# A recurrence with two gated feed-forward layers: TensorE's order in the first three chunks written as a timetable

## The chip, the core and the metric

The kernel runs on one core of a Trainium2 chip. TensorE (PE) multiplies matrices, PEld loads its weights, VectorE (DVE), ScalarE (ACT) and GpSimd (POOL) do the elementwise work, and SyncE (SP) issues the DMAs. Each engine works through its own instructions in a fixed order, which is set when the kernel is built. The metric is the time of one execution in microseconds (us).

## What is computed

The attention part is a recurrence over 768 steps for each of 4 batches x 8 heads, with a 40 x 40 state. It is followed by two gated layers over 3072 tokens (320 to 1536 to 320), all in fp32:

```python
for t in range(S):
    y[:, :, t] = np.einsum('bhd,bhde->bhe', rt, state)
    Sa = np.einsum('bhde,bhe->bhd', state, at)
    state_decay = state * wt[:, :, None, :] - np.einsum('bhd,bhe->bhde', Sa, bt)
    state = state_decay + np.einsum('bhd,bhe->bhde', vt, kt)
...
g = x @ w_gate; val = x @ w_val
x = (g * sigmoid(g)) * val @ w_out          # first layer
x = sigmoid(x @ w_gate) * (x @ w_val) @ w_out   # second layer, its own weights
```

## The kernel before

The recurrence is cut into 12 chunks of 64 steps, and all 32 heads of a chunk are worked on together. A chunk m goes through these stages, each a Python generator whose `yield`s mark its steps:

- `prep_a(m)`: the decay products of the chunk's steps. For chunks 0 to 3 they are scans on DVE, transposed on PE (`dtp`, L153) and copied out (`pn`, L404); for chunk 0 this is in `first()`. Later chunks read them from DRAM, where `powers` has put them. Then the scaled a is transposed (`tp` L356, copied to `lq` at L456), and four **key groups** follow: transposition `tp` L356, ACT's copy `kbt` L467, the key products `kps` L471, ACT's copies into `bn` L480 and L481, DVE's masked copy into `lq` L483.
- `prep_b(m)`: the inverse of a unit triangular matrix from `bn`. For chunks 0 to 2 it is `halves`: DVE solves 16-row blocks (L539 to L564) and PE joins them (`hps` L573, L586); for later chunks it is `whole`: DVE solves 32-row blocks (L497 to L521), and the result X goes through DRAM (`xd`, written at L524, read back at L526). In both PE joins the blocks of 32 by `zps` L626 and `xps` L642.
- `chain(m)`: the serial part, state to state: `qps` L677 (behind it POOL clears `lq` again, L687), `ups` L695, `sps` L706 and DVE's update of the state `sT`. It needs the inverse of chunk m and the state of chunk m - 1.
- `post(m)`: the chunk's output: `aps` L749, the mask `am` L757, `yps` L775, `ysb` L785. `cp(m)` is `chain(m)` and then `post(m)`.
- `extra(m, ys)`: the first feed-forward layer (FFN) on the finished block m: the input x (`xtp` L930), `gv` L984, activation `g` on ACT (L988), `hh` on ACT (L992), `hl` on POOL (L993), `po` L1002. Block 0 uses three of the weight tiles ("w tile 0" to "w tile 2"), later blocks five; the rest of the first layer and all of the second follow behind the recurrence. `extra(-2)` prepares w tiles 0 to 2, `extra(0)` also tiles 3 and 4 (`load_w`: DMA, ACT L882, POOL, DVE, and the ACT conversion L902).
- `powers(n)`: decay products for chunks 4 to 7 and 8 to 11. DVE clamps (L231), POOL multiplies (L228: two tiles `wp` and `wq`), and DMAs write both to DRAM (`pd`, `rd`). These two tiles lie in the same buffers as w tiles 3 and 4.

`fill()` zeroes static buffers on ACT; `marks` and `behind` put one instruction behind another of the same engine; `ends_scan` gives the chunk's total decay (`pend`). What sets the order before: `merge` draws steps from the generators by rates and offsets (QA, QB, NA, NB and so on), which gives the program's order, and the Tile scheduler then orders each engine's instructions from that order and its own estimates of when operands are ready.

## Time and profile before

| | |
|---|---|
| time, median of 3 runs | 1327.23 us (1326.39 to 1330.4) |
| the profiled execution | 1332.88 us, span 1331.2 us |
| PE busy | 1243.8 us, 93% of the span |
| DVE, ACT, POOL busy | 763.1, 598.3, 558.5 us |
| PE's mean granted clock | 0.938 |

The profile's page gives sums over the span and the span in 40 slices of 33.3 us. The views of the trace give groups of instructions, waits and timelines. L153 is line 153 of the kernel before; times are us from the start of the span. In a timeline a row is a run of equal instructions: start, length, engine, line, operation, out <- in, shape, count, and in brackets how long the engine had stood idle ahead of it and what released it. In the trace a matrix product in fp32 appears as two instructions.

### The profile page before, as it was taken

The page shows a single profiled execution, that of the slowest core. Times are in us where ns is not written, and L with a number is a line of the kernel's source. Part 1 is how long each engine was busy: PE and PEld are TensorE (multiplying, and loading weights), DVE is VectorE, ACT ScalarE, POOL GpSimd, SP SyncE. Part 2 cuts the span into 40 slices and gives each one's busy share as a digit, 9 for nine tenths or more (in the row PEclk, how much of TensorE's full clock was granted, in tenths as well). Part 3 has the DMA queues.
Part 4 walks back from the last instruction along what each step waited for, and adds up shares of the span by engine and source line. Part 5 has one row for each costly group of instructions (what it writes and reads, how often), then busy time and mean ns, then how long its engine had stood idle before and what let it go on. Part 6 is the DMA issues. An engine that isn't in the chain of part 4 may idle for free.

```text
span 1331.2 us, 34568 instructions
## 1 busy us (share of the span) xinstructions
PE 1243.8 (93%) x14209; PEld 1182.1 (89%) x14209; DVE 763.1 (57%) x1578; ACT 598.3 (45%) x1446; POOL 558.5 (42%) x767
## 2 busy tenths in 40 slices
PE   5577799999999999999899999999999999999996
PEld 4476688888888888988899999999999999999996
DVE  6768567776786678877889888733122122212221
ACT  8453464456555655655434444423333333333331
POOL 5657341222322223447777888723222222222221
PEclk7666687899999999999899999999999999999998
DMA  6644923335424533344355544221000000000000
GB/s 211 125 124 127 214 84 99 88 105 154 121 80 110 154 109 82 103 129 124 111 188 185 181 155 161 89 85 51 23 23 23 23 23 23 23 23 23 11 11 14
DMA packets 153065, 126.15 MB, mean 95 GB/s; under 512 B 100929, under 2 KB 131137, under 8 KB 152641
## 3 DMA queue, kind: packets, MB, share of 16 engines
q1 hardware_dynamic: 152896, 123.84, 32.9%
q8 instruction: 114, 1.87, 0.6%
q14 instruction: 55, 0.44, 0.1%
HBM read 92.05 MB, written 31.76 MB: 93 GB/s over the span
## 4 chain that ended last, share of the span: by engine, by line
PE 69%; DVE 14%; DMA 5%; ACT 4%; issue 3%; POOL 2%; SPq 1%; DVEq 0%; ACTq 0%; POOLq 0%
PE g L984 26%; PE po L1002 16%; PE gv L984 8%; PE tp L356 3%; PE aps L749 3%; PE kps L471 3%; PE yps L775 2%; DVE dt L887 2%; DVE ds L892 1%; DMA wt<-in_a_w_dram 1%; PE qps L677 1%; PE ups L695 1%; PE xps L642 1%; PE sps L706 1%; DVE part L517 1%
## 5 line engine op out<-in xcount | busy, mean ns | idle before, releaser
L984 PE MATMUL g<-x,w 128*128 128x256 f32 x3520 | 489.7, 282 | 2.1 <-DVE g L990 1.3
L984 PEld LDWEIGHTS g<-x,w 128*128 128x128 f32 x3520 | 458.9, 190 | 4.2 <-DVE g L990 2.1
L993 POOL TENSOR_TENSOR hl<-g,hh 128x256 fp32r<-128x256 f32 x288 | 218.9, 760 | 474.3 <-ACT hh L992 430.9
L991 DVE TENSOR_TENSOR g<-g,g 128x256 f32<-128x256 f32 x220 | 93.0, 423 | 308.2 <-PE g L984 298.6
L992 ACT CAST hh<-g 128x256 fp32r<-128x256 f32 x288 | 117.0, 406 | 268.3 <-DVE g L991 246.9
L1002 PE MATMUL po<-w,hh 128*128 128x320 f32 x1152 | 225.8, 312 | 3.6 <-ACT hh L992 3.5
L1002 PEld LDWEIGHTS po<-w,hh 128*128 128x128 f32 x1152 | 175.3, 189 | 5.3 <-ACT hh L992 4.6
L984 PE MATMUL gv<-x,w 128*128 128x256 f32 x1088 | 161.0, 298 | 3.2 <-ACT x L936 1.7
L984 PEld LDWEIGHTS gv<-x,w 128*128 128x128 f32 x1088 | 143.2, 199 | 7.1 <-ACT x L936 2.0
L1002 PE MATMUL po<-w,hl 128*128 128x320 f32 x576 | 142.0, 316 | 0.0
L988 ACT ACTIVATE g<-g 128x256 f32<-128x256 f32 x220 | 84.2, 383 | 128.4 <-PE g L984 117.4
L904 POOL TENSOR_TENSOR dt<-dt,w 128x384 f32<-128x384 f32 (+1 forms) x72 | 79.4, 1103 | 77.8 <-DVE ds L891 36.5
L1002 PEld LDWEIGHTS po<-w,hl 128*128 128x128 f32 x576 | 91.7, 189 | 1.4 <-POOL hl L993 0.5
L511 DVE TENSOR_TENSOR pr<-part,sn 128x4 f32<-128x4 f32 (+4 forms) x135 | 74.7, 553 | 3.0
L471 PE MATMUL kps<-lq,kbt 104*128 104x128 f32 x384 | 62.0, 312 | 8.1 <-DVE lq L483 6.9
L517 DVE TENSOR_REDUCE part<-pr 128x2 f32<-128x4 f32 (+4 forms) x135 | 66.8, 495 | 3.4
L483 DVE TENSOR_TENSOR lq<-kps,part 64x256 f32<-64x256 f32 x96 | 40.4, 421 | 46.2 <-ACT bn L481 43.7
L471 PEld LDWEIGHTS kps<-lq,kbt 104*128 104x128 f32 x384 | 54.1, 217 | 10.9 <-issue 7.1
L356 PE MATMUL tp<-ident,part 128*104 128x128 f32 x288 | 50.7, 298 | 12.9 <-ACT pend L168 6.7
L749 PE MATMUL aps<-rbd,ut 104*128 104x128 f32 x384 | 57.1, 292 | 3.6 <-DVE am L757 2.0
L902 ACT CAST w<-dt 128x384 fp32r<-128x384 f32 (+1 forms) x72 | 35.6, 495 | 54.3 <-DVE dt L887 47.3
L480 ACT ACTIVATE bn<-kps 32x256 f32<-32x256 f32 x96 | 35.8, 373 | 53.6 <-PE kps L471 44.1
(171 smaller groups left out, 1788.9 us busy)
## 6 DMA issues: line engine op xcount, KB each, us to landing
raw<-in_w_dram SPq DMA_DIRECT2D x48, 384.0 KB
xd<-x SPq DMA_DIRECT2D x12, 896.0 KB
x<-xd SPq DMA_DIRECT2D x12, 896.0 KB
raw<-in_w_dram SPq DMA_DIRECT2D x24, 320.0 KB
ld<-in_a_kb_dram SPq DMA_DIRECT2D x22, 320.0 KB
ld<-rd SPq DMA_DIRECT2D x32, 160.0 KB
pn<-pd SPq DMA_DIRECT2D x32, 160.0 KB
ld<-in_a_a_dram SPq DMA_DIRECT2D x12, 320.0 KB
```

Source lines behind the costliest of these rows:

```text
L356: t = nc.tensor.transpose(ps[0 : x.shape[1], n, :], x, ident)
L471: nc.tensor.matmul(kps[:, n].rearrange("p h t -> p (h t)"), lhsT=kbt[0:PW, n, :], rhs=lq[m % 3][0:PW, 4 * g4 + n].rearrange("p h t -> p (h ...
L511: nc.vector.tensor_tensor(out=o, in0=xs[:, 0:kk, None, 0:n].to_broadcast([P, kk, 2, n]), in1=sn[:, None, n : n + 2, 0:n].to_broadcast([P, ...
L517: nc.vector.tensor_reduce(out=xs[:, 0:kk, n : n + 2], in_=o, axis=AX.X, op=ALU.add)
L749: nc.tensor.matmul(aps[:, n, h2], lhsT=ut[0:PW, x, 2 * h2 : 2 * h2 + 2].rearrange("p u s -> p (u s)"), rhs=rbd[0:PW, x, h2].rearrange("p b ...
L904: sub(out=tf, in0=tf, in1=w.bitcast(F32), op=ALU.subtract)
L984: nc.tensor.matmul(gv[n], lhsT=p, rhs=q, start=e == 0, stop=e == len(seq) - 1)
L988: nc.scalar.activation(out=g, in_=gv[0], func=AF.Sigmoid)
L991: nc.vector.tensor_tensor(out=g, in0=gv[1], in1=g, op=ALU.mult)
L992: nc.scalar.copy(out=hh, in_=g)
L993: self.heng.tensor_tensor(out=hl, in0=g, in1=hh.bitcast(F32), op=ALU.subtract)
L1002: self.nc.tensor.matmul(ops[u], lhsT=p[:, us], rhs=q, start=first and n == 0, stop=last and n == 2)
```

## The change

The first three chunks' work on PE is no longer ordered by `merge` and the scheduler, but by a script of steps (A is `prep_a`, B `prep_b`, C `cp`, W and E the two `extra`s, P the powers; "A0:3" is three steps of A0), inside which PE keeps the order of the program. From chunk 2's `cp` on the loop with its rates goes on as before. Around it:

- of the zero fills only five are made at the start (`lq0`, `qv`, `lq1`, `sT`, `x16`), the others behind chunk 0's last copy into `bn`;
- chunk 0's `pend` product moves out of `first()` into `prep_a(0)`;
- the transposition of the next key group is queued ahead of the products of this one, `kbt` takes turns with a second pair of buffers in chunks 0 and 1, and the key products take turns over several PSUM banks: four in chunk 0, three in chunk 1, two in chunk 2, one (`mm`) from chunk 3 on; `banks()` hands out the bank `pg` too;
- chunk 0 leaves out the copies and the eight transpositions of its state, which is zero;
- in `halves` two small scalings move from ACT to DVE;
- the first of the two groups of powers has its clamps behind chunk 0's block solve.

```diff
-    def fill():
-        for t in fills:
-            nc.scalar.copy(out=t, in_=zero[(slice(None),) + (None,) * (len(t.shape) - 2)].to_broadcast(t.shape))
-        fills.clear()
+    def fill(ts, mark=None):
+        for t in ts:
+            to = nc.scalar.copy(out=t, in_=zero[(slice(None),) + (None,) * (len(t.shape) - 2)].to_broadcast(t.shape))
+            if mark:
+                behind(to, mark)
...
-    def ends_scan(m, p, ps):
+    def end_rows(p):
         nc.vector.tensor_tensor(
             out=pairs(pe)[:, 0].rearrange("p h (j c) -> p h j c", c=4),
             in0=p[:, None, :, C : C + 1].to_broadcast([P, 2, 10, 4]),
             in1=cm[:, :, None, :].to_broadcast([P, 2, 10, 4]),
             op=ALU.mult,
         )
+
+    def ends_scan(m, ps):
         nc.tensor.matmul(ps[0:PW], lhsT=pe[:, 0], rhs=hot, start=True, stop=True)
...
-            ends_scan(0, p, pt)
+            end_rows(p)
...
-            behind(clamp, "keys")
+            if n == 1:
+                behind(clamp, ("solved", 0))
...
+    early = ("lq0", "qv", "lq1", "sT")
+    fill([fills[n] for n in early] + [x16])
...
+        if m == 0:
+            ends_scan(0, ptp.tile([P, 4, P], F32, tag="tp", name="pep")[:, 0, 0:NS])
         bn = wk.tile([P, NS, C], F32, tag="bn", name="bn", bufs=2)
+        keys = {0: ((pmm, "mm"), (pzy, "zy"), (po, "po1"), (pqu, "qu")), 1: ((pmm, "mm"), (po, "po1"), (pg, "gv")), 2: ((pmm, "mm"), (pg, "gv"))}
+        keys = keys.get(m, ((pmm, "mm"),))
+        turned = tr4(lambda n: tk[:, n])
         for g4 in range(4):
             q = slice(4 * g4, 4 * g4 + 4)
-            ps = tr4(lambda n: tk[:, 4 * g4 + n], ("joined", None, "merged", None)[g4] if m == 1 else None)
-            kbt = wk.tile([P, 4, P], F32, tag="kbt", name="kbt", bufs=1)
-            nc.scalar.copy(out=kbt[0:PW], in_=ps[0:PW])
-            pool, tag = ((pmm, "mm"), (pzy, "zy"), (pqu, "qu"), (po, "po1"))[g4 if m == 0 else 0]
+            tag = "am" if m < 2 and g4 % 2 else "kbt"
+            kbt = wk.tile([P, 4, P], F32, tag=tag, name="kbt", bufs=2 if tag == "am" else 1)
+            nc.scalar.copy(out=kbt[0:PW], in_=turned[0:PW])
+            if g4 < 3:
+                turned = tr4(lambda n: tk[:, 4 * g4 + 4 + n])
+            pool, tag = keys[g4 % len(keys)]
...
-                nc.scalar.mul(out=bn[hi, q, 0:32], in_=kps[hi, :, h2, 32:64], mul=-1.0)
+                marks["keys"] = nc.scalar.mul(out=bn[hi, q, 0:32], in_=kps[hi, :, h2, 32:64], mul=-1.0)
...
-        nc.scalar.mul(out=sn, in_=full[:, :, 0:16], mul=par[:, 0:1])
+        nc.vector.tensor_scalar(out=sn, in0=full[:, :, 0:16], scalar1=par[:, 0:1], scalar2=None, op0=ALU.mult)
...
-        nc.scalar.mul(out=x16.rearrange("p r t -> p (r t)")[:, 1:256:34], in_=nk, mul=-1.0)
+        nc.vector.tensor_scalar(
+            out=x16.rearrange("p r t -> p (r t)")[:, 1:256:34], in0=nk, scalar1=-1.0, scalar2=None, op0=ALU.mult
+        )
...
-            nc.vector.tensor_scalar(out=to(0), in0=src, scalar1=sel[:, z : z + 1], scalar2=None, op0=ALU.mult)
+            marks[("solved", m)] = nc.vector.tensor_scalar(out=to(0), in0=src, scalar1=sel[:, z : z + 1], scalar2=None, op0=ALU.mult)
...
+            if m:
+                for h2 in range(2):
+                    nc.scalar.copy(out=two(Q[E40[h2], h2, sg]), in_=pairs(sT, s4)[E40[h2]])
+
+                ps = tr4(lambda n: sT[:, 4 * hb + n])
+                nc.scalar.copy(
+                    out=sd[0:PW, s4], in_=ps[0:PW].rearrange("p n (h e) -> p n h e", h=2)[..., 0:D]
+                )
...
-    merge([(prep_a(0), 1, 0)])
-    fill()
-    for t, step in ((x16, 17), (xs, 34)):
-        t = t.rearrange("p r t -> p (r t)")[:, ::step]
-        nc.gpsimd.tensor_copy(out=t, in_=odd[:, 0:1].to_broadcast([P, 16]) if step == 34 else less.to_broadcast([P, 16]))
-    nc.gpsimd.memset(tkb[2][..., D:64], 0.0)
-    start = [(prep_b(0), *QB)]
-    if NCH > 1:
-        start.append((prep_a(1), *QA))
-    merge(start)
-    for m in range(NCH + 1):
+    tokens = {
+        **{f"A{m}": prep_a(m) for m in range(4)},
+        **{f"B{m}": prep_b(m) for m in range(3)},
+        **{f"C{m}": cp(m) for m in range(2)},
+        "W": extra(-2, out),
+        "E": extra(0, out),
+        "P": all_powers(),
+    }
+
+    def run(script):
+        for x in script.split():
+            name, _, n = x.partition(":")
+            for _ in range(int(n or 1)):
+                next(tokens[name], None)
+
+    with tc.manual_schedule(engines={mybir.EngineType.PE}):
+        run("A1 A0:3 A1 A0 A1 A0 A1 A0:2 A1")
+        fill([t for n, t in fills.items() if n not in early], "keys")
+        for t, step in ((x16, 17), (xs, 34)):
+            t = t.rearrange("p r t -> p (r t)")[:, ::step]
+            nc.gpsimd.tensor_copy(
+                out=t, in_=odd[:, 0:1].to_broadcast([P, 16]) if step == 34 else less.to_broadcast([P, 16])
+            )
+        nc.gpsimd.memset(tkb[2][..., D:64], 0.0)
+        run("C0:3 A2 A1:2 B0:3 A1:5 B0 A2 B0 A2 B0 A2 B0:2 A2 C0:4")
+        run("A2 C0 A2 C0 A2 C0 A2 C0 A2 C0 A2:2 C0:3 A3 B1:3 C1:3 B1:2 W:10 P:99 B1:3 E C1:4 B2:3")
+        run("E C1 E C1 E C1 E C1:4 A3:4 B2:5 A3:9 E:19")
+    for m in range(2, NCH + 1):
         todo = []
-        if m == 0:
-            todo.append((extra(-2, out), *QW))
-            if len(groups) > 1:
-                todo.append((all_powers(), *QP))
-        if 0 <= m < NCH:
-            todo.append((cp(m), *(NP if m else QN)))
-        if 0 <= m < NCH - 1:
-            todo.append((prep_b(m + 1), *(NB if m else QC)))
-        if 2 <= m + 2 < NCH:
-            todo.append((prep_a(m + 2), *(NA if m else QD)))
-        todo.append((ahead(m), *(NX if m > 0 else QX)))
+        if m < NCH:
+            todo.append((cp(m), *NP))
+        if m < NCH - 1:
+            todo.append((prep_b(m + 1), *NB))
+        if m + 2 < NCH:
+            todo.append((prep_a(m + 2), *NA))
+        todo.append((ahead(m), *NX))
```

What stands in PE's queue around chunk 0's join (hps; in both kernels lq0 and bn of this place are chunk 0's, tkb1 and lq1 chunk 1's). Before:

```order
L356 MATMUL tp_628<-ident_58,part0_88 104x128 x4
L356 MATMUL tp_635<-ident_58,part0_88 104x128 x4
L573 MATMUL hps_325<-x1t_373,bn_227 32x16 x64
L586 MATMUL hps_325<-part1_212,pr_327 16x16 x64
L356 MATMUL tp_643<-ident_58,tkb1_90 104x128 x4
L356 MATMUL tp_661<-ident_58,tkb1_90 104x128 x4
L626 MATMUL zps_539<-x1t_536,bn_227 32x32 x32
L471 MATMUL kps_650<-lq1_210,kbt_648 128x128 x4
```

The same place now:

```order
L358 MATMUL tp_456<-ident_58,part0_88 104x128 x4
L358 MATMUL tp_494<-ident_58,tkb1_90 104x128 x4
L358 MATMUL tp_501<-ident_58,tkb1_90 104x128 x4
L479 MATMUL kps_506<-lq1_190,kbt_499 128x128 x4
L358 MATMUL tp_519<-ident_58,tkb1_90 104x128 x4
L479 MATMUL kps_524<-lq1_190,kbt_517 128x128 x4
L358 MATMUL tp_537<-ident_58,tkb1_90 104x128 x4
L479 MATMUL kps_542<-lq1_190,kbt_535 128x128 x4
L479 MATMUL kps_555<-lq1_190,kbt_553 128x128 x4
L583 MATMUL hps_463<-x1t_486,bn_244 32x16 x64
```

All four key groups of chunk 1 have moved ahead of chunk 0's hps.

The key groups of chunk 3 (lq0 and tkb0 again) in PE's queue, and chunk 2's inverse (hps_1739 before). Before, the last of the four groups:

```order
L749 MATMUL aps_2074<-rbd_199,ut_198 128x128 x4
L356 MATMUL tp_2494<-ident_58,part0_88 104x128 x4
L471 MATMUL kps_1957<-lq0_192,kbt_1955 128x128 x4
L365 MATMUL pep_2501<-ident_58,part2_86 104x16
L775 MATMUL yps_2146<-part3_197,rbd_199 64x40 x16
L775 MATMUL yps_2146<-tkb1_90,am_2063 64x40 x8
L775 MATMUL yps_2146<-tkb1_90,am_2079 64x40 x8
L573 MATMUL hps_1739<-x1t_2043,bn_1064 32x16 x64
```

Now, the end of chunk 2's inverse and the first group:

```order
L634 MATMUL zps_2209<-x1t_2206,bn_959 32x32 x32
L650 MATMUL xps_2244<-part1_208,zt_2208 32x32 x32
L358 MATMUL tp_2279<-ident_58,part0_88 104x128 x4
L358 MATMUL tp_2286<-ident_58,part0_88 104x128 x4
L702 MATMUL ups_2686<-qs_2684,part1_208 64x40
L702 MATMUL ups_2745<-qs_2743,part1_208 64x40
L702 MATMUL ups_2686<-qs_2684,part1_208 64x40 x15
L358 MATMUL tp_2294<-ident_58,tkb0_89 104x128 x4
L702 MATMUL ups_2745<-qs_2743,part1_208 64x40 x4
L358 MATMUL tp_2301<-ident_58,tkb0_89 104x128 x4
L702 MATMUL ups_2745<-qs_2743,part1_208 64x40 x11
L713 MATMUL sps_2765<-part3_195,tkb2_91 40x40
```

Chunk 3's groups stood ahead of chunk 2's hps and now begin behind chunk 2's xps; the products of the first follow directly on the last row.

ACT's queue around the first conversion of w tile 3 (w8_2311 before, w8_2369 now). Before:

```order
L480 ACTIVATE bn_1064<-kps_1126 32x256
L481 ACTIVATE bn_1064<-kps_1126 32x4x32
L902 CAST w8_2311<-dt_2314 128x384
L540 ACTIVATE sn_1740<-sn_1740,part2_86 128x256
L600 ACTIVATE part1_212<-hps_1140 16x16x16 x2
L404 COPY pn_1615<-dtp_1621 128x16x32
```

Now:

```order
L1008 ACTIVATE g_1813<-gv_1796 128x256
L747 COPY ut_196<-tp_1823 104x4x2x64
L1012 CAST hh_1814<-g_1813 128x256
L1008 ACTIVATE g_1853<-gv_1836 128x256
L922 CAST w8_2369<-dt_2372 128x384
L1012 CAST hh_1854<-g_1853 128x256
L1008 ACTIVATE g_1891<-gv_1874 128x256
```

The conversion has moved from between the solves of chunks 1 and 2 to between two steps of block 0's FFN.

## Rows read from the trace of the kernel before

**Rows 1.** The page: busy tenths and granted clock of PE in 40 slices.

```profile
PE   5577799999999999999899999999999999999996
...
PEclk7666687899999999999899999999999999999998
```

**Rows 2.** Windows: length, busy time (instructions) of the engines, PE's clock, DMA share, GB/s.

```profile
core 0: us, PE busy (x) PEld busy (x) DVE busy (x) ACT busy (x) POOL busy (x), PEclk, DMA share, GB/s
...
40.00:90.00 50.00, 31.76 (x637) 27.74 (x638) 32.45 (x66) 24.82 (x56) 28.26 (x38) 0.59 0.70 158
90.00:170.00 80.00, 58.87 (x960) 52.13 (x957) 57.36 (x116) 36.48 (x83) 46.46 (x57) 0.66 0.61 150
170.00:212.00 42.00, 38.52 (x728) 35.97 (x727) 30.42 (x69) 22.39 (x54) 16.98 (x24) 0.75 0.37 105
...
264.00:316.00 52.00, 50.05 (x763) 44.97 (x763) 39.30 (x79) 30.51 (x75) 14.81 (x20) 1.00 0.47 129
```

**Rows 3.** Waits of PE from 0 to 212: total us, times, longest.

```profile
PE dtp L153 <- ACT pn L404: 8.0, 2, 5.7
...
PE tp L356 <- ACT pend L168: 6.7, 1, 6.7
```

**Rows 4.** Timeline of PE in chunk 0 and chunk 1's keys.

```profile
23.31 1.92 PE L471 MATMUL kps<-lq,kbt 104*128 104x128 f32 x8
...
33.87 1.16 PE L471 MATMUL kps<-lq,kbt 104*128 104x128 f32 x8
...
54.11 1.90 PE L573 MATMUL hps<-x1t,bn 16*32 16x16 f32 x128 [9.19 <-DVE x1t L563]
...
73.03 2.05 PE L471 MATMUL kps<-lq,kbt 104*128 104x128 f32 x8 [2.85 <-DVE lq L483]
...
83.63 1.67 PE L706 MATMUL sps<-part,tkb 128*40 128x40 f32 x46
...
85.93 1.06 PE L471 MATMUL kps<-lq,kbt 104*128 104x128 f32 x8
```

**Rows 5.** Timeline of PE from chunk 1's inverse to chunk 3's.

```profile
121.28 0.75 PE L573 MATMUL hps<-x1t,bn 16*32 16x16 f32 x66
124.83 2.05 PE L471 MATMUL kps<-lq,kbt 104*128 104x128 f32 x8 [2.79 <-DVE lq L483]
...
142.13 1.12 PE L153 MATMUL dtp<-ident,s 128*64 128x128 f32 x8 [5.70 <-ACT pn L404]
...
168.56 0.81 PE L706 MATMUL sps<-part,tkb 128*40 128x40 f32 x32
...
184.99 1.06 PE L471 MATMUL kps<-lq,kbt 104*128 104x128 f32 x8
...
190.98 1.91 PE L573 MATMUL hps<-x1t,bn 16*32 16x16 f32 x128 [2.79 <-DVE lq L483]
...
209.04 1.92 PE L642 MATMUL xps<-part,zt 32*32 32x32 f32 x64
...
249.99 0.69 PE L642 MATMUL xps<-part,zt 32*32 32x32 f32 x32
```

**Rows 6.** Timeline of DVE: a powers' reciprocal, and chunk 3's whole solve.

```profile
127.44 0.40 DVE L246 RECIPROCAL part<-wp 128x40 f32<-128x40 f32 x1 [2.76 <-POOL wp L228]
...
190.76 1.23 DVE L497 STREAM_TRANSPOSE sn<-bn 128x1024 f32<-128x1024 f32 x1
...
200.85 0.69 DVE L505 TENSOR_TENSOR nt<-sn 128x512 f32<-128x512 f32 x1
...
221.58 0.71 DVE L521 STREAM_TRANSPOSE x1t<-part 128x512 f32<-128x512 f32 x1
```

**Rows 7.** Timeline of ACT: the first conversion of w tile 3.

```profile
139.76 0.51 ACT L902 CAST w<-dt 128x384 fp32r<-128x384 f32 x1 [5.06 <-issue]
```

**Rows 8.** Groups of POOL, 17 to 170: busy us, mean ns of one.

```profile
L228 POOL TENSOR_TENSOR wp<-wp 128x320 f32<-128x320 f32 x28 | 27.9, 997 | 2.1 <-DVE wp L231 1.4
```

**Rows 9.** Timeline of SP's queue: issue times of chunk 3's round trip.

```profile
227.30 1.31 SPq L524 DMA_DIRECT2D xd<-part  x2
232.21 2.01 SPq L526 DMA_DIRECT2D part<-xd  x4
```

More of the change, by code (lines that the diff above doesn't have):

```diff
@@ L53, in attention @@
     dr = ctx.enter_context(tc.tile_pool(name="at_dram", bufs=2, space=DRAM))
-    room, fills = {}, []
+    room, fills = {}, {}
     def static(shape, name, val=None, part=None):
@@ L74, in static @@
         if val == 0.0:
-            fills.append(t)
+            fills[name] = t
         elif val is not None:
@@ L263, in all_powers @@
             yield from powers(n)
-    lq = [static([P, NS, 2, C], "lq0", 0.0)]
-    fill()
+    lq = [static([P, NS, 2, C], f"lq{i}", 0.0) for i in range(3)]
     mask = static([P, C], "mask", 1.0, "part2")
@@ L355, in tr4 @@
             x = get(n)
-            t = nc.tensor.transpose(ps[0 : x.shape[1], n, :], x, ident)
-            if n == 0 and name:
-                behind(t, name)
+            nc.tensor.transpose(ps[0 : x.shape[1], n, :], x, ident)
         return ps
@@ L585, in halves @@
                 at = 32 * (j % 2) + 16
-                last = nc.tensor.matmul(
+                nc.tensor.matmul(
                     ps[32 * j : 32 * j + 16, q, 16:32],
@@ L593, in halves @@
                 )
-        if m == 0:
-            marks["joined"] = last
         for j in (0, 2, 1, 3):
@@ L641, in prep_b @@
                 lo, hi = slice(64 * h2, 64 * h2 + 32), slice(64 * h2 + 32, 64 * h2 + 64)
-                last = nc.tensor.matmul(
+                nc.tensor.matmul(
                     ps[lo, q],
@@ L649, in prep_b @@
                 )
-        if m == 0:
-            marks["merged"] = last
         for h2 in range(2):
@@ L665, in half @@
             sg, s4 = slice(8 * hb, 8 * hb + 8), slice(4 * hb, 4 * hb + 4)
-            for h2 in range(2):
-                nc.scalar.copy(out=two(Q[E40[h2], h2, sg]), in_=pairs(sT, s4)[E40[h2]])
-            ps = tr4(lambda n: sT[:, 4 * hb + n])
-            nc.scalar.copy(
-                out=sd[0:PW, s4], in_=ps[0:PW].rearrange("p n (h e) -> p n h e", h=2)[..., 0:D]
-            )
+            if m:
[5 more added lines that the diff above has]
+                )
             qps = pool.tile([P, 8, D], F32, tag=tag, name="qps")
```

20 lines of the change are left out of this document (8 added, 12 removed).

## The prediction

> **What bounds the kernel now.** I read the page's slices first: TensorE (PE) is nearly always busy and at full clock, except in the first five slices by its busy share and the first seven by its clock [rows 1]. The windows put figures to that: PE is busy for 31.8 of the 50 us from 40 to 90 at a granted clock of 0.59, for 58.9 of the 80 us from 90 to 170 at 0.66, for 38.5 of the 42 up to 212 at 0.75, and from 264 on for 50 of 52 at 1.00 [rows 2]. So the change works on the only stretch with much idle time in it, and what it brings forward by about 250 us is kept to the end, since PE has work all the time behind that. The list of waits names what PE stood for in that stretch: the decays' copy pn from ScalarE (ACT) 8.0 us, the first `tp` 6.7 [rows 3]; the longest single one is 9.19 us for the first inverse's x1t from VectorE (DVE) [rows 4]. The timelines of PE, DVE, ACT and SyncE (SP) give the milestones that I shift below. The profiled execution took 1332.88 us (span 1331.2 and 1.68 around it), 5.65 us over the median of 1327.23; I work out a shift in its time and apply it to the median.
>
> **The shift is read at one place:** chunk 3's last inverse product, xps, which PE starts at 249.99 us [rows 5]. Up to there both orders have the same chunks, key groups and feed-forward (FFN) tiles ahead of it to within about 3 us of PE work, which I count as zero and keep for the range.
>
> **1. Chunk 0.** Before, chunk 1's first transpositions are done at 54.11 − 9.19 = 44.9 and PE idles until hps starts at 54.11 [rows 4]. The timetable places chunk 1's four key groups into that hole, ahead of hps. Chunk 0's own four groups took from 23.31 to 35.03, so 11.7 us at the low clock [rows 4]; from 46 on that ends at 58 to 63, and hps starts 4 to 9 us later than before. x1t itself comes earlier, since two scalings move from ACT to DVE and the powers' clamps wait for the solve (my guess: 49 instead of 54), but this no longer decides. In return hps to the end of sps holds no key group any more. It took from 54.11 to 85.30, 31.2 us, and in it lay three key products of 2.05 us, one with a 2.85 us wait, and two dozen transpositions, about 6 us by the same half clock [rows 4]: 15 us, which leaves 16; chunk 2's decay transpositions, now inside, give 6 to 10 of it back. Chunk 0's state is then done at 80 to 89, for 85.3: nothing gained, but chunk 1's keys are complete 24 us earlier (58 to 63 for 87 [rows 4]). The other edits here (smaller fills, eight transpositions of a zero state left out) act on the 6.7 us that PE waits for the first `tp` [rows 3]; they are worth 0 to 3 us at the front, covered by the same hole, and without that cover at most these 3 us; I count nothing.
>
> **2. Chunk 2's keys, then chunk 1.** The timetable finishes chunk 2's keys right behind chunk 0's state, at about 110 (four groups of 4 to 5 us from 90 on). Before, they lay between chunk 1's products: chunk 1's hps starts at 121.28 and its sps ends at 169.37, 48.1 us [rows 5]. In this lay two of the key products (2.05 us, one with a 2.79 us wait), some 8 us of decay transpositions with their 5.70 us wait [rows 5], and some 8 us of FFN and of chunk 3's keys: 28 to 30 us, so about 19 without, of which I take 22 to 26. With hps at 115, sps ends at 137 to 141, some 30 us earlier. This is the large gain of the change.
>
> **3. FFN of block 0 and the rest of chunk 1.** These now run by themselves, and three engines' queues stand in their way. On POOL the first `hl` stands behind 27 of the 29 multiplications of the second group of powers. These can't start before chunk 1's qps, since the clearing of lq1 behind qps stands ahead of them in POOL's queue (about 116); 27 of 1.0 us [rows 8] end at 143. On ACT the conversion of w tile 3 stands between two steps of the FFN, and it waits for the DMAs that write the first powers' tile out of the same buffer. Before, it started at 139.76, 12.3 us after the reciprocal that ends this tile (127.44), with ACT idle for 5.06 us ahead of it [rows 6, 7]. That tile is now done 21 multiplications behind 116, at 137 to 145 with other work between them, and the conversion runs at 150 to 158; everything behind it on ACT (the second `hh`, chunk 1's copies) waits, and PE with it. On SP, chunk 2's load of v stands behind the same writes. From there one and a half FFN tiles, the output copies and chunk 1's second half are left, some 15 us of PE work at the low clock: 165 to 173, I take 171. Of the 30 us gained, up to half is lost here.
>
> **4. Chunk 2's inverse.** hps to xps took from 190.98 to 210.96, 20.0 us, with other products inside [rows 5]; by itself, the waits between its products now open, 12 to 16. It is done at 183 to 187: 24 to 28 us earlier than before.
>
> **5. Chunk 3's keys, the step that decides.** Before, chunk 3's four key groups lay between chunk 1's state and block 0's FFN and were done at 186.05 [rows 5]; DVE began chunk 3's whole solve at 190.76 [rows 6]. The timetable places them behind chunk 2's xps. They have one PSUM bank, so each group goes transposition, ACT copy, product, ACT and DVE copies in turn. At the pace of chunk 0 (11.7 us and the last mask) this is 14 us: the solve starts at 199 to 203, which is **8 to 12 us later** than before, although everything ahead of it is 24 to 28 us earlier. With a 2.79 us wait, as at 124.83 [rows 5], at three of the groups it would be 207 to 211.
>
> From there to X: before, L497 at 190.76, the last transposition at 221.58, the write to DRAM issued at 227.30, the reads issued until 234.22 [rows 6, 9]: 43.5 us. In this lie 8.9 us in which L505 waited (from 191.99 to 200.85 [rows 6]) and 5 in which SP's queue held the write back; both can go, neither must. So 30 to 44, and the landing; I take 40. With a start at 201, X is there at 241, and xps can run 9 us before its 249.99: **−9**.
>
> **The rivals.** *A, the forecast:* X decides, and two thirds of the lead are handed back: −4 to −20. *B, the lead goes entirely:* the solve starts at 205 to 212 and X takes 41 to 45 us: 246 to 254, within 4 us of before. For it: no step ahead of 190 speeds this solve, and one bank serves all four groups. *C, slower:* the powers, the conversion behind their DMA writes and the FFN behind the conversion slip in a row. It decides from a solve start later than 213 on (213 + 41 is 4 us behind 249.99). If lq1 is cleared at 128 instead of 116, each later step slips by 12, the solve starts at 211 to 215 and X is there 43 to 45 us later, at 254 to 260; with the mask waits of 8 us on top, at 268 at worst. I price it at **+4 to +15**. For it: ACT, POOL and SP work off their queues in order, and the trace shows this very stall (5.06 us [rows 7]). Against it: the first group of powers, 29 multiplications of 1.0 us [rows 8] behind the solve at 49 and the weights' work between them, is out of POOL's way by about 90. *D, a larger gain:* the solve's two idle spans go, X takes 31 us and isn't waited for, and PE closes up. Before, PE needed 39 us from the end of chunk 2's xps to chunk 3's xps (210.96 to 249.99 [rows 5]); with chunk 3's keys added, some 9 us, 48 from 185 on gives 233: −17, and up to −25 where the denser stretch runs at the higher clock. PE's stretches with the higher busy share show the higher clock (0.59 at 64%, 0.66 at 74%, 0.75 at 92% [rows 2]), and a key product takes 2.05 us in the one and 1.06 in the other [rows 4]. [...] *E, the order isn't what the script says:* the instruction order of the changed kernel shows the moves on PE, so it has no chance of its own.
>
> **How the numbers follow.** A 0.44, B 0.20, C 0.24, D 0.12. The median less 9 gives 1318. The range goes up to 1338 (C's +11) and down to 1302 (D's −25), which leaves a little under 0.2 outside. About 0.3% (4 us) is what a measurement of this kernel can tell from no change: faster 0.56 (A and D), same 0.20 (B), slower 0.24 (C).
>
> **What would show it.** Step 1: no 9 us hole ahead of hps, and chunk 1's four kps there. Step 2: chunk 1's sps done by about 140. Step 3: ACT idle ahead of the conversion of w tile 3, at 150 to 158, and PE waiting for `hh` or `hl`. Step 5: chunk 3's L497 at 199 to 203, and a wait of PE ahead of xps at about 241. I am wrong if the solve starts before 195 or after 213, if xps isn't waited for, or if time is lost or won behind 264, where only the phase of the queues changes.

## The result

The changed kernel takes 1344.89 us (median of 4 runs, 1343.2 to 1350.69) against 1328.82 us for the kernel before (4 runs, 1326.39 to 1330.45): a ratio of 1.013 with a 95% interval of 1.0093 to 1.0167, so 16 us slower. The forecast was 1318, and its range ended at 1338. The profiled execution of the changed kernel took 1345.87 us, span 1344.1; its span is 12.9 us longer than before's.

The page of the changed kernel, the busy tenths and the granted clock of PE in 40 slices of 33.6 us:

```profile
PE   6666876899999999999889999999999999999996
...
PEclk8658677989999999999999999999999999999998
```

Each digit of the first line is PE's busy share of a slice in tenths, of the second its granted clock. Over the first five slices the two kernels are much alike [rows 1], but PE stays below 9 in the sixth to eighth, where it had been at 9. The windows show this in us (columns as in [rows 2]):

```profile
40.00:90.00 50.00, 32.02 (x654) 28.91 (x654) 42.95 (x86) 26.72 (x62) 32.08 (x38) 0.60 0.31 84
90.00:170.00 80.00, 56.51 (x999) 52.08 (x1000) 42.24 (x81) 32.90 (x73) 49.29 (x63) 0.72 0.69 154
170.00:212.00 42.00, 30.71 (x746) 27.05 (x744) 15.08 (x35) 18.59 (x42) 16.10 (x22) 0.72 0.54 164
212.00:264.00 52.00, 42.07 (x445) 37.27 (x445) 42.04 (x96) 27.96 (x68) 12.90 (x17) 0.87 0.27 80
264.00:316.00 52.00, 49.73 (x666) 43.76 (x666) 38.24 (x79) 25.58 (x63) 11.25 (x16) 0.87 0.35 98
```

The one window of before that is needed beside these and isn't among [rows 2]:

```profile
212.00:264.00 52.00, 50.10 (x665) 45.12 (x664) 38.03 (x73) 26.47 (x66) 9.39 (x13) 0.88 0.28 76
```

From 170 to 212 PE is idle for 11.3 us (42 − 30.71; before 3.5), from 212 to 264 for 9.9 us (before 1.9). These 15.8 us are new. Behind 264 another 5.9 us of idle time is new, most of it between 628 and 732 (11.6 for 8.3). With 1.2 us more up to 170, PE is idle for 22.9 us more in the whole span (110.2 for 87.3).

The span is only 12.9 us longer, because PE's busy time fell by 10.0 us, from 1243.8 to 1233.8. PE has the same instructions to work through but for the eight transpositions left out (14201 for 14209 in the trace). What the windows show to differ is the granted clock, and in the kernel before one key product took 2.05 us and another 1.06 [rows 4], at a granted clock of 0.50 (73.0 to 75.1 us) and of 1.00 (85.9 to 87.0). Up to 170 us, before and then changed:

```profile
0.00:170.00 170.00, 115.48 (x1876) 102.14 (x1877) 117.84 (x238) 92.67 (x193) 98.23 (x135) 0.67 0.63 159
```

```profile
0.00:170.00 170.00, 114.31 (x1941) 104.24 (x1942) 114.52 (x240) 87.11 (x179) 95.19 (x133) 0.71 0.56 139
```

PE gets through more instructions here in about the same busy time, at a clock of 0.71 for 0.67; the idle time is no shorter (55.7 us for 54.5). Counted by the work that is left (PE's busy time over the span less its busy time so far), 1119.5 us are left at 170, for 1128.4 before. So at 170 us the changed kernel is 8.9 us ahead, at the higher clock and without less waiting; at 212 it is 1.0 ahead (1088.8 for 1089.8), and at 264 it is 7.1 behind (1046.8 for 1039.7). A part of these 7.1 us may be the clock again: from 264 to 316 it is 0.87, where it was 1.00 before [rows 2].

The milestones on PE (start, length, what was waited for; line numbers are always those of the kernel that ran):

```profile
57.93 1.27 PE L583 MATMUL hps<-x1t,bn 16*32 16x16 f32 x128
...
85.58 2.51 PE L713 MATMUL sps<-part,tkb 128*40 128x40 f32 x64 [3.39 <-ACT part L707]
...
117.69 1.74 PE L583 MATMUL hps<-x1t,bn 16*32 16x16 f32 x128
...
130.12 2.06 PE L634 MATMUL zps<-x1t,bn 32*32 32x32 f32 x64 [5.68 <-DVE x L568]
...
143.07 2.51 PE L713 MATMUL sps<-part,tkb 128*40 128x40 f32 x64 [2.68 <-ACT part L707]
...
153.27 2.08 PE L756 MATMUL aps<-rbd,ut 104*128 104x128 f32 x8 [3.76 <-ACT ut L747]
...
179.63 1.27 PE L583 MATMUL hps<-x1t,bn 16*32 16x16 f32 x128
...
189.81 1.92 PE L650 MATMUL xps<-part,zt 32*32 32x32 f32 x64 [1.26 <-ACT zt L644]
...
202.82 2.08 PE L479 MATMUL kps<-lq,kbt 104*128 104x128 f32 x8 [1.23 <-ACT kbt L473]
...
261.52 0.88 PE L650 MATMUL xps<-part,zt 32*32 32x32 f32 x44
```

Chunk 0's hps, its sps, chunk 1's hps and its sps answer to 54.11, 83.63 [rows 4], 121.28 and 168.56 [rows 5]: chunk 1's state is ready at 145.6, 23.8 us earlier than before. Chunk 2's hps and xps come 11.4 and 19.2 us earlier (190.98 and 209.04 [rows 5]), but chunk 3's xps at 261.52 for 249.99, 11.5 us later. Between them lies chunk 3's solve on DVE, which begins 31.2 us later than before (190.76 [rows 6]):

```profile
221.95 1.23 DVE L505 STREAM_TRANSPOSE sn<-bn 128x1024 f32<-128x1024 f32 x1
...
254.03 0.67 DVE L529 STREAM_TRANSPOSE x1t<-part 128x512 f32<-128x512 f32 x1
```

### The profile page after: what moved, and what is told of

Its sections match the earlier page's. It is cut to its first block, busy times and chain, and to the rows that moved or that the text cites. A ratio compares the mean times of both kernels' runs of the same rounds, so it can differ in the third digit from the quotient of the medians.

```text
span 1344.1 us, 34525 instructions
## 1 busy us (share of the span) xinstructions
PE 1233.8 (92%) x14201; PEld 1176.1 (88%) x14201; DVE 761.0 (57%) x1584; ACT 595.1 (44%) x1434; POOL 559.9 (42%) x767
## 4 chain that ended last, share of the span: by engine, by line
PE 72%; DVE 11%; DMA 5%; ACT 4%; POOL 3%; issue 3%; SPq 1%; POOLq 0%; ACTq 0%; DVEq 0%
PE g L1004 29%; PE po L1022 17%; PE gv L1004 7%; PE yps L782 3%; PE tp L358 3%; PE aps L756 3%; PE kps L479 2%; PE qps L684 2%; DMA wt<-in_a_w_dram 2%; PE ups L702 2%; POOL wp L231 1%; PE xtp L950 1%; DVE dt L907 1%; PE xps L650 1%; DVE ds L912 1%
## 5 line engine op out<-in xcount | busy, mean ns | idle before, releaser
L1004 PE MATMUL gv<-x,w 128*128 128x256 f32 x1088 | 157.3, 295 | 7.1 <-DVE g L1011 4.3
L756 PEld LDWEIGHTS aps<-rbd,ut 104*128 104x128 f32 x384 | 50.1, 200 | 13.5 <-ACT ut L747 8.7
L912 DVE SCALAR_TENSOR_TENSOR ds<-raw,ds 128x384 f32<-128x384 uint32 (+1 forms) x72 | 58.6, 815 | 1.4
```

The lines of the kernel that those rows point to most:

```text
L756: nc.tensor.matmul(aps[:, n, h2], lhsT=ut[0:PW, x, 2 * h2 : 2 * h2 + 2].rearrange("p u s -> p (u s)"), rhs=rbd[0:PW, x, h2].rearrange("p b ...
L912: nc.vector.scalar_tensor_tensor(out=sg.bitcast(F32), in0=lo.bitcast(U32), scalar=2.0**-52, in1=sg.bitcast(F32), op0=ALU.mult, op1=ALU.mult,)
L1004: nc.tensor.matmul(gv[n], lhsT=p, rhs=q, start=e == 0, stop=e == len(seq) - 1)
```

## The experiments

Each was run in rounds with the kernel before on the same chip. The medians of before in them lie between 1328.2 and 1329.7. All times below are medians; "ratio" is against the kernel before, with its 95% interval. The edits are shown in short; "..." stands for what is left out.

### Does the late solve set the time?

Theory 1: the late start of chunk 3's solve makes the kernel slower. Theory 2: PE loses its time in many waits of the fixed order, whichever of them comes first. The first experiment puts chunk 3's keys ahead of chunk 2's inverse:

```diff
-... 2: ((pmm, "mm"), (pg, "gv"))}
+... 2: ((pmm, "mm"), (pg, "gv")), 3: ((pg, "gv"),)}
-        run("E C1 E C1 E C1 E C1:4 A3:4 B2:5 A3:9 E:19")
+        run("E C1 E C1 E C1 E C1:4 A3:13 B2:5 E:19")
```

> The changed kernel with one edit of the script: chunk 3's key groups come ahead of chunk 2's inverse (A3:13 B2:5 in place of A3:4 B2:5 A3:9); since chunk 2's inverse then still holds the bank mm, they use the bank gv. In the changed kernel chunk 3's solve starts at 221.95 us, 31 us later than before, and xps of chunk 3 at 261.5 for 250. Theory 1 (the late start of this solve sets the time): the solve starts at 195 to 205, xps of chunk 3 by 245, and the time falls by 10 to 20 us, to 1325 to 1335. Theory 2 (the time is lost in the many small waits of PE's fixed order, whatever comes first): chunk 2's inverse and its state slip by the same 15 us or so, and the time stays at 1341 to 1349.

Measured: 1343.07 us, ratio 1.0099 (1.0082 to 1.0116). The solve did start earlier, at 206.23 (theory 1 had asked for 195 to 205), but chunk 3's xps came at 256.32, 5.2 us earlier and not by 245, and the time fell by only 1.8 us. The windows of this kernel and its chunk 2 inverse, which now comes behind the keys, show where it went:

```profile
170.00:212.00 42.00, 28.93 (x511) 25.28 (x511) 17.56 (x40) 19.42 (x47) 17.19 (x22) 0.66 0.59 164
212.00:264.00 52.00, 48.25 (x676) 42.73 (x677) 46.25 (x101) 26.54 (x62) 11.37 (x15) 0.79 0.27 75
```

```profile
208.36 1.56 PE L596 MATMUL hps<-part,pr 32*16 32x16 f32 x128 [1.62 <-ACT pr L591]
212.38 1.92 PE L634 MATMUL zps<-x1t,bn 32*32 32x32 f32 x64 [2.47 <-DVE x1t L612]
215.56 1.92 PE L650 MATMUL xps<-part,zt 32*32 32x32 f32 x64 [1.25 <-ACT zt L644]
```

The idle time from 212 to 264 fell from 9.9 to 3.8 us, but from 170 to 212 it rose from 11.3 to 13.1, and chunk 2's xps slipped from 189.81 to 215.56. The work left at 264 is 1047.0 us, the same as in the changed kernel (1046.8). So an earlier solve alone doesn't reach xps or the end, and theory 1 in this form falls, as far as a run can tell that missed both of its milestones.

The second experiment asks what held chunk 3's keys. In ACT's queue the preparation of w tiles 3 and 4 stood between them; here it is put behind the last of them:

```diff
-            nc.scalar.activation(out=t.bitcast(F32), ...)
+            first = nc.scalar.activation(out=t.bitcast(F32), ...)
+            if LATE:
+                LATE[0](first)
...
-        run("... B2:5 A3:9 E:19")
+        run("... B2:5 A3:9")
+        LATE.append(lambda inst: behind(inst, "keys"))
+        run("E:19")
+        LATE.clear()
```

> The changed kernel, but the preparation of w tiles 3 and 4 is put behind chunk 3's last copy into bn on ACT. In the changed kernel its steps stand between chunk 3's key copies in ACT's queue and wait for POOL there (3.75 us at 193.51, 2.12 at 201.75). Theory 1a (these steps hold chunk 3's keys): the first key product of chunk 3 comes at about 196 for 202.8, the solve starts at 208 to 214 for 221.95, and the time falls by 8 to 14 us, less what block 1's FFN then waits for tile 3. Theory 1b (the one PSUM bank and the handoffs of a group set the pace): the solve starts no more than 3 us earlier, and the time is the same within 4 us.

Measured: 1348.23 us, ratio 1.0143 (1.0125 to 1.0161), 3.3 us slower than the changed kernel. The first key product of chunk 3 came at 200.40 and the solve began at 219.12, 2.8 us earlier. That is theory 1b: not the weights' steps but, by elimination, the handoffs within and ahead of the groups.

### Which part of the script costs the time?

```diff
 # shorter script: up to chunk 1's inverse
-        run("... W:10 P:99 B1:3 E C1:4 B2:3")
-        run("E C1 E C1 E C1 E C1:4 A3:4 B2:5 A3:9 E:19")
+        run("... W:10 P:99 B1:3")
+    merge([(tokens["C1"], *NP), (tokens["B2"], *NB), (tokens["A3"], *NA), (tokens["E"], *NX)])
```

> The changed kernel with the timetable only up to chunk 1's inverse; chunk 1's chain and output, chunk 2's inverse, chunk 3's keys and block 0's FFN are merged by the rates of before and ordered by the scheduler. Theory 1: chunk 3's keys move forward among them, the solve starts at 185 to 205, and the time falls by 15 to 30 us below the changed kernel's 1345, to 1315 to 1330; the lead of the first two chunks is then kept in part. Theory 2: it stays above 1340.

Measured: 1325.7 us, ratio 0.997 (0.9958 to 0.9981): 19 us faster than the changed kernel, and a little faster than before.

Then the script one piece longer, so that only its last line is merged:

```diff
-        run("E C1 E C1 E C1 E C1:4 A3:4 B2:5 A3:9 E:19")
+    merge([(tokens["C1"], *NP), (tokens["B2"], *NB), (tokens["A3"], *NA), (tokens["E"], *NX)])
```

> The changed kernel with the script kept up to the first steps of chunk 2's inverse; only its last line (block 0's FFN, chunk 1's output, the rest of chunk 2's inverse, chunk 3's keys) is merged by the rates of before and ordered by the scheduler. With the script kept a little shorter the time was 1325.7. Theory 2a: 1323 to 1332, since the cost sits in the last line. Rival (the line before it costs the larger part, by chunk 2's keys and chunk 1's chain in a row): 1336 to 1346.

Measured: 1353.22 us (1351.04 to 1362.94), ratio 1.0197 (1.0156 to 1.0238), slower even than the changed kernel. Both sides of the expectation are missed, and this is what told most. The two kernels differ by the piece "E C1:4 B2:3" in the script: chunk 1's chain and the first steps of chunk 2's inverse, in a row. The windows from 90 to 170, first of the kernel with the shorter script, then of this one:

```profile
90.00:170.00 80.00, 72.48 (x1031) 66.44 (x1032) 45.42 (x95) 42.51 (x99) 47.36 (x60) 0.66 0.75 182
```

```profile
90.00:170.00 80.00, 55.15 (x1008) 50.62 (x1008) 43.76 (x85) 34.19 (x78) 47.73 (x60) 0.77 0.74 167
```

PE is idle there for 7.5 us in the one and 24.9 in the other. In the faster one the scheduler had put chunk 3's keys (kps) and block 0's FFN (gv) between the steps of chunk 1's chain (ups, sps); PE's timeline there:

```profile
142.04 1.93 PE L702 MATMUL ups<-qs,part 64*64 64x40 f32 x28
143.90 2.07 PE L479 MATMUL kps<-lq,kbt 104*128 104x128 f32 x8
...
152.00 1.91 PE L479 MATMUL kps<-lq,kbt 104*128 104x128 f32 x8
153.84 0.50 PE L713 MATMUL sps<-part,tkb 128*40 128x40 f32 x8
154.27 2.43 PE L1004 MATMUL gv<-x,w 128*128 128x256 f32 x12
```

In the slower one chunk 1's ups and sps stand in a row and the first of these key products comes at 165.76. Chunk 3's solve began at 168.86 in the faster one, for 203.24 in the slower.

The next one moves other independent work into the later gaps, block 0's FFN tiles:

```diff
-        run("E C1 E C1 E C1 E C1:4 A3:4 B2:5 A3:9 E:19")
+        run("C1 C1 C1 C1:4 A3:4 B2 E B2 E B2:3 A3:2 E A3 E A3:6 E:19")
```

> The changed kernel with one edit of the script's last line: block 0's three FFN tiles no longer run through chunk 1's output but between the steps of chunk 2's inverse and chunk 3's key groups. Theory 2a (PE loses its time where dependent steps stand in a row with no independent work between them, the solve of chunk 3 not alone): the idle time from 170 to 264 falls, and the kernel falls to 1330 to 1340 from 1345. Rival (the gaps only move into chunk 1's output, whose FFN filler is gone): 1343 to 1350.

Measured: 1350.81 us, ratio 1.0163 (1.0142 to 1.0185): the rival, 0.8 us over its range. The idle time from 90 to 170 rose from 23.5 to 25.6 us, from 170 to 264 it fell from 21.2 to 17.7, and the solve began later still, at 224.51. Filling a gap with work that was filling another one gained nothing here.

Now the place of chunk 3's preparation alone, with the rest of the script as it was: its decay transpositions between the products of chunk 1's inverse, its key groups between those of chunk 1's chain.

```diff
-C0:3 A3 B1:3 C1:3 B1:2 W:10 P:99 B1:3 E C1:4 B2:3
-E C1 E C1 E C1 E C1:4 A3:4 B2:5 A3:9 E:19
+C0:3 A3 B1:3 C1:3 A3 B1:2 A3 W:10 P:99 B1 A3 B1 A3 B1 E A3 C1 A3 C1 A3:2 C1 A3:2 C1 A3:9 B2:3
+E C1 E C1 E C1 E C1:4 B2:5 E:19
```

> The changed kernel with only the place of chunk 3's preparation changed in the script: its decay transpositions go between the products of chunk 1's inverse, its key groups between those of chunk 1's chain, ahead of chunk 2's inverse. In the changed kernel PE is idle for 23.5 us from 90 to 170, where chunk 1's inverse and chain stand in a row with nothing between them, and for 21 us from 170 to 264, where chunk 2's inverse and chunk 3's keys do. Theory 2b (idle time in both stretches, because independent work stands behind dependent work instead of between it): the solve of chunk 3 starts at 165 to 180 for 222, PE idles 8 to 15 us less up to 264, and the time is 1325 to 1335. Rival (any order fixed by hand loses here, since PE waits for whichever is late): 1341 to 1350.

Measured: 1333.96 us, ratio 1.0047 (1.0031 to 1.0062): 10.9 of the 16 us are gone. The solve began at 173.24, and the windows are

```profile
90.00:170.00 80.00, 54.32 (x920) 47.48 (x922) 44.00 (x88) 36.36 (x85) 48.62 (x60) 0.66 0.80 185
170.00:212.00 42.00, 33.15 (x739) 30.33 (x735) 27.62 (x61) 18.63 (x41) 19.25 (x27) 0.83 0.42 123
212.00:264.00 52.00, 51.52 (x693) 45.88 (x692) 43.79 (x84) 27.49 (x67) 10.61 (x14) 0.87 0.30 83
```

From 170 to 264 PE is idle for 9.3 us, for 21.2 in the changed kernel. From 90 to 170 nothing is gained: 25.7 us for 23.5, since in the fixed order the chain of chunk 1 now waits behind keys that wait themselves:

```profile
158.18 2.05 PE L479 MATMUL kps<-lq,kbt 104*128 104x128 f32 x8 [5.38 <-DVE lq L491]
160.16 1.30 PE L713 MATMUL sps<-part,tkb 128*40 128x40 f32 x32
...
167.76 2.05 PE L479 MATMUL kps<-lq,kbt 104*128 104x128 f32 x8 [2.60 <-DVE lq L491]
169.74 1.30 PE L713 MATMUL sps<-part,tkb 128*40 128x40 f32 x32
```

Its last sps stands at 169.74, for 143.07 in the changed kernel. Up to 264 PE's idle time fell by 6.2 us in all, less than the 8 to 15 that I expected. Of the 13.5 us by which the span is shorter than the changed kernel's, 6.8 are idle time and 6.6 PE's busy time (1227.2 for 1233.8 us for the same 14201 instructions, at a mean granted clock of 0.942 for 0.939). That this second half of the gain comes from the clock is argued and not shown. The waits above are where the remaining 5 us over before are likeliest to sit; no run took them away, so this last step is argued and not shown.

And the script as the program's order, with the scheduler free to place PE's instructions:

```diff
-    with tc.manual_schedule(engines={mybir.EngineType.PE}):
+    if True:
```

> The changed kernel with the script as it stands giving the program's order, but the scheduler free to order PE's instructions by its estimates of readiness, as it does for the other engines. Theory 2b (the fixed place of each step on PE, with nothing to slip into a gap): 1320 to 1334, most of the 25 us between the changed kernel and the one without the timetable. Rival (the program's order, which sets the priorities of ACT, DVE, POOL and the DMAs too, costs it): 1339 to 1350.

Measured: 1337.26 us, ratio 1.0063 (1.0046 to 1.008), 7.6 us less than with PE's order fixed and 3 us over the range that I gave it. The idle time up to 170 fell from 55.7 to 45.1 us, but the solve still began at 219.94, and from 212 to 264 8.8 us of idle time stayed. So it takes both: PE's fixed order costs some 8 us, and the program's order the 17.7 us from here to the kernel without the timetable (next section). That chunk 3's late keys are what costs in that order is argued.

### The timetable and the other edits apart

```diff
 # all edits but the timetable
-    with tc.manual_schedule(engines={mybir.EngineType.PE}):
-        run(...)
+    merge([(prep_a(0), 1, 0)])
+    ... fills, then merge and loop with the rates of before
```

> All of the change but the timetable: fills, banks, queued transpositions, the two scalings on DVE, the skipped zero state, with the steps merged by the rates of before. Theory 1 (the timetable's order costs the time): 1320 to 1333, near the kernel before. Rival (the other edits cost it, the held clamps or the fills above all): 1338 to 1350, as the changed kernel.

Measured: 1319.61 us, ratio 0.9932 (0.9915 to 0.9948): 10 us faster than before and 25 us faster than the changed kernel. The timetable costs the time. PE is idle for 83.2 us of this span, 27.0 less than in the changed kernel.

> The kernel before with the timetable alone: none of the other edits (fills, banks, queued transpositions, DVE scalings, skipped state, held clamps); the two marks that put chunk 1's transpositions behind chunk 0's products, which the timetable replaces, are left out. If the timetable's cost stands by itself, it is some 25 us as between the changed kernel and the one without the timetable: 1348 to 1360. If the timetable costs only together with the edits (the held clamps, which start the powers late): 1325 to 1338.

Measured (edit: the loop and merges of before replaced by the script, and the two marks left out): 1379.9 us, ratio 1.0372 (1.0355 to 1.039). That is beyond both sides of the expectation: the timetable costs 50 us on the kernel before and 25 us with the other edits beside it. What PE waits for in it, from 0 to 264 (total, times, longest):

```profile
PE sps L706 <- ACT part L700: 15.0, 3, 8.0
PE kps L471 <- ACT kbt L467: 14.7, 10, 4.7
PE kps L471 <- DVE lq L483: 11.6, 5, 3.5
```

Ten times a key product waits for ACT's copy of its own transposition, five times for DVE's masked copy, which reads the bank. The banks and the queued transpositions are there for the timetable.

Which of the other edits gains without it? Three runs took one each away from the kernel with all but the timetable. In the second the key groups are as before except for the two marks, which stay left out in all of these kernels:

```diff
 # without the hold
-            if n == 1:
-                behind(clamp, ("solved", 0))
 # key groups as before: in-group transposition, one kbt, banks of before
-        turned = tr4(lambda n: tk[:, n])
+            ps = tr4(lambda n: tk[:, 4 * g4 + n])
 # scalings back on ACT
-        nc.vector.tensor_scalar(out=sn, ...)
+        nc.scalar.mul(out=sn, ...)
```

> All of the change but the timetable, and without the hold of the first powers' clamps behind chunk 0's solve. All of the change but the timetable gave 1319.6, 10 us under the kernel before; in it chunk 0's join starts at 46.2 us for 54.1 and chunk 3's solve at 168.9 for 190.8. If the hold gives this (chunk 0's solve on DVE free of the clamps, of 1.5 us each, and of POOL's multiplications): chunk 0's join back at 50 to 54 and the time at 1325 to 1331. If it is the other edits (fills, banks, queued transpositions, skipped zero state): 1316 to 1322.

> All of the change but the timetable (1319.6), with the key groups as before: each transposition queued in its own group, one kbt buffer, one bank from chunk 1 on. If the banks and the queued transpositions give the 10 us that the edits gain without the timetable: chunk 1's keys end near 87 us for 64.7, and the time is 1326 to 1331. If not: 1317 to 1323.

> All of the change but the timetable (1319.6), with the two small scalings of the block solve back on ACT. If they are a part of the gain (ACT's queue holds them up, as before at 139.76, where the conversion ahead of them waited 5.06 us): chunk 0's join at 49 to 54 us for 46.2, the time 1322 to 1330. If not: 1317 to 1323.

Measured: 1320.76 (ratio 0.9938, 0.9915 to 0.9962), 1314.16 (0.9895, 0.9872 to 0.9917) and 1317.13 (0.9929, 0.9913 to 0.9946). None of the three carries the gain. In the first and the third, chunk 0's hps did go back (to 54.33 and 53.05, from 46.18), and the time didn't follow. 1314.16 is the fastest kernel of this study, 14 us under before and 31 under the changed kernel.

Then single edits on the kernel before, and what is left when two are undone together:

```diff
 # fills alone: five early, the others behind chunk 0's last copy into bn
+    early = ("lq0", "qv", "lq1", "sT")
+    fill([fills[n] for n in early] + [x16])
 # zero state alone
+            if m:
 # two undone together: key groups as before and scalings on ACT
```

> The kernel before with the fills alone: five early, the others behind chunk 0's last copy into bn. All of the change but the timetable gave 1319.6, and 1314.2 with the key groups as before, 1317.1 with the scalings on ACT, 1320.8 without the hold of the powers. If the fills give the gain: 1314 to 1322, with chunk 0's keys done by 32 us for 35. If they only shorten ACT's queue at the front: 1325 to 1330.

> The kernel before with the copies and the eight transpositions of chunk 0's zero state left out, and nothing else. By its own work this is worth under 2 us, since PE idles behind it anyway: 1326 to 1330. If leaving them out lets PE, ACT and the rest of the program fall into another order (as the scheduler fills differently from there on): 1314 to 1324, or above 1332.

> All of the change but the timetable, with the key groups as before and the scalings on ACT: what is left is the fills, chunk 0's pend product, the skipped zero state and the hold of the powers. If the two undone edits cost their 5 and 2 us independently: 1308 to 1314, the fastest of all. If each of these differences is only another order of the scheduler: 1312 to 1322.

Measured: 1347.17 (ratio 1.0118, 1.0102 to 1.0135), 1323.58 (0.9966, 0.9947 to 0.9984) and 1333.91 (1.0024, 0.9998 to 1.005). None is where a sum of effects would put it: the fills alone cost 17 us, the eight left-out transpositions and their copies gain 6, and undoing two edits together loses 14, though undone alone one gained 5 and the other nothing clear of the noise (ratio 0.9929 for 0.9932). With the scheduler free, each of these edits also gave another order: chunk 3's solve begins at 190.76 in the kernel before, at 193.35 with the fills alone, at 179.29 without the zero state and at 180.93 with the two undone. That it is this order which is measured, and not the edit's own work, is argued: no run held the order and changed one edit. Which single edit gives the 10 us stays open (the two left-out marks, which no run put back, among them).

### What tells the kernels apart

PE has little idle time behind 264 us (27 to 42). So I take from each profile PE's busy time over the span less its busy time up to 264: the work that is left there. This is bookkeeping and no cause, since the span is 264 us, this work and the idle time behind 264. It also holds what the clock may add: over the same instructions, but for the eight transpositions, PE's busy time goes from 1222 us (scalings back on ACT, mean granted clock 0.952) to 1261 us (timetable alone, 0.914) in these kernels.

| kernel | PE work left at 264 us | chunk 3's xps starts | PE idle in the span | span |
|---|---|---|---|---|
| key groups as before, no timetable | 1017.4 | 232.7 | 84.5 | 1310.8 |
| all but the timetable | 1020.5 | 237.7 | 83.2 | 1314.0 |
| shorter script | 1027.7 | 244.3 | 82.6 | 1322.7 |
| chunk 3's preparation moved | 1033.9 | 252.3 | 103.4 | 1330.6 |
| before | 1039.7 | 250.0 | 87.3 | 1331.2 |
| the changed kernel | 1046.8 | 261.5 | 110.2 | 1344.1 |
| chunk 3's keys early | 1047.0 | 256.3 | 105.4 | 1341.9 |
| FFN tiles moved | 1050.1 | 267.4 | 113.1 | 1349.1 |
| timetable alone | 1081.8 | 302.1 | 121.4 | 1382.3 |

Span less work left is 291 to 301 in all of these and in the other kernels too, except the one with the fills alone, where it is 306 (14.4 us idle from 316 to 628). So it tells kernels apart to some 10 us, and not the changed kernel from the one with the early keys. The start of chunk 3's xps does as well: the span less it is 1076 to 1086 in all kernels but two (1096 with only the last line merged, 1100 with the fills alone). The start of chunk 3's solve doesn't: it is 206 in the kernel with the early keys (1341.9) and 191 in the kernel before, and from it to xps are 39.6 us in the changed kernel, 50.1 with the early keys, 59.2 before and 79.1 with chunk 3's preparation moved.

## Why the prediction was wrong

**Step 1** held: hps at 57.93 (58 to 63 forecast), no hole ahead of it, chunk 0's state at 88.1 (80 to 89), chunk 1's keys done at 58.0.

**Step 2** held in kind: chunk 2's keys done at 111.8 (110), chunk 1's hps at 117.69 (115). The term that was mis-sized is hps to sps: 27.9 us, not 22 to 26. Where I had taken the other work out, waits appeared in its place: 5.68 us ahead of zps and 2.68 ahead of sps in the rows above, and 3.1 within hps, for which the profile names no cause. The wait ahead of zps wasn't all chunk 1's own. In DVE's queue the clamps of the second powers stood ahead of the copy (L610) that leads to zps:

```profile
125.38 1.49 DVE L234 TENSOR_SCALAR wp<-wq 128x2560 f32<-128x2560 f32 x1 [6.18 <-issue]
126.91 1.49 DVE L234 TENSOR_SCALAR wq<-wq 128x2560 f32<-128x2560 f32 x1
128.31 0.84 DVE L610 TENSOR_SCALAR part<-hps 16x256 f32<-16x256 f32 x2
```

The products that L610 reads ended at 124.45, so it began 3.9 us late. The load of these powers was issued at 116.73, for 81.58 before, behind the first group's writes of the same tile (from 101.11 on, for 69.91 before). I had counted the hold of the first group's clamps as a gain for chunk 0's solve only. Most likely it is what made all of this late; no run took it away with the timetable in place.

**Step 3** came out late, chunk 2's hps at 179.63 for 165 to 173, and by another way than I had said. The conversion of w tile 3 wasn't waited for, since it ran only when ACT had stood for `gv`:

```profile
158.80 0.38 ACT L1008 ACTIVATE g<-gv 128x256 f32<-128x256 f32 x1 [4.70 <-PE gv L1004]
159.08 0.50 ACT L922 CAST w<-dt 128x384 fp32r<-128x384 f32 x1
```

The second group of powers began at 127.02 and not at 116, behind the same late clamps (8.03 us of POOL's idle time), and the `hl` that I had made the bound ran at 154.17, early enough. PE stood for chunk 1's output instead, 3.76 us for the copy ut.

**Step 4** held in its length, 12.1 us (12 to 16). It ended at 191.7 (183 to 187), since it began late.

**Step 5 is the one that failed**, and twice. First in size: I let the first group follow xps at once and take 14 us for all four. In fact the first product came 11 us behind the end of xps. Up to it ACT's queue worked off the lq copies (195.94, four of 0.59 us) and chunk 2's ups copies, with stops for POOL:

```profile
201.75 0.54 ACT L902 ACTIVATE dt<-raw 128x384 f32<-128x384 f32 x1 [2.12 <-POOL w L930]
202.19 0.57 ACT L473 COPY kbt<-tp 104x512 f32<-104x512 f32 x1
```

Then the groups took 19 us. The solve began at 221.95, some 21 us later than the 201 of the forecast and beyond my worst bound of 211: 6.7 us came from the steps ahead, 11 from the wait for the first product and 3 from the groups. Putting the weights' steps away won 2.8 us only, so what else held the first product stays open. The 40 us from there to X held: xps came 39.6 us behind the solve's start.

Second in kind: I made this solve the place that decides and PE's wait for X the loss. PE didn't stand for X (no idle time ahead of 261.52), and with the solve begun 16 us earlier xps came 5.2 us earlier and the time fell by 1.8. What the runs showed in its place is PE's idle time in many waits from 170 to 264 (15.8 us more than before), between steps that wait for each other. Before, chunk 1's output stood between the products of chunk 2's inverse [rows 5]:

```profile
194.56 1.91 PE L749 MATMUL aps<-rbd,ut 104*128 104x128 f32 x8
196.40 0.90 PE L586 MATMUL hps<-part,pr 32*16 32x16 f32 x84
197.26 2.08 PE L749 MATMUL aps<-rbd,ut 104*128 104x128 f32 x8
```

The timetable had done this work, and block 0's FFN, by 175 us. Moving chunk 3's preparation in between dependent steps took back 10.9 of the 16 us. The prediction's reading that both orders have the same work ahead of chunk 3's xps says nothing of what stands next to what, and that was the trap. Reading the shift at chunk 3's xps was no mistake: it gave +11.5 us there and +12.9 in the span, and the place holds in nearly all kernels.

Of **the rivals**, C had the sign, nearly the size (+4 to +15; the median moved by +16), its condition (a solve later than 213) and a part of its way: the powers slipped by 11 us, through the late clamps and not through a late clearing of lq1, but neither `hl` nor the conversion of w tile 3 was waited for. D's premise, that a denser order brings a higher clock, had no support: from 90 to 170 the clock was 0.66 at 91% busy (shorter script) and 0.84 at 82% (all but the timetable), and its two key products of 2.05 and 1.06 us [rows 4] lie in one and the same stretch, 40 to 90. So no run shows the clock's part of D's −25. Yet the clock did move: the 8.9 us of lead at 170 came with 0.71 for 0.67. The edits counted at zero were worth 10 us without the timetable and 35 with it (1379.9 us with the timetable alone). The chances gave 0.24 to a slower kernel; the range should have reached further on that side, since step 5's own worst bound rested on the pace of one chunk.

## What to carry to other kernels

Where one engine is busy from some point on to the end, measure a change of order at that point, by the work that this engine has left or by a milestone at the end of the changed stretch. Milestones inside the stretch can mislead: here chunk 1's state came 23.8 us earlier and chunk 2's xps 19.2, and the kernel got slower. An order that finishes chains early spends the independent work that later handoffs need as cover; before moving a stage forward, ask what will stand between the dependent steps that it leaves behind. An order fixed on one engine still meets the queues of the others, as with the clamps on DVE. In this program, ordered by a scheduler, the effects of small edits didn't add, so each has to be measured in the place where it will stand.

## What was not expected of the hardware

The granted clock didn't follow the busy share of a long window: from 90 to 170 us the rows above show 0.66 at 72.48 of 80 us busy and 0.77 at 55.15, and the kernel with all but the timetable shows

```profile
90.00:170.00 80.00, 65.40 (x1200) 59.34 (x1199) 51.72 (x102) 44.42 (x104) 50.58 (x64) 0.84 0.65 176
170.00:212.00 42.00, 36.49 (x637) 32.17 (x630) 32.79 (x70) 19.27 (x46) 20.54 (x26) 0.59 0.57 142
```

with 0.84 at 82% and then 0.59 at 87%. So in these kernels the busy share of such a stretch is no guide to its clock, and a gain priced by it, as in rival D, isn't supported.
